# Attention with 16 queries per head: TensorE's loop turned to QK(g), PV(g-1), a K block transposed during the first softmax, no closing barrier, last rows stored by two queues

## The chip, the cores and the metric

The kernel runs on one core of one Trainium2 chip. The time is the device time of one execution in microseconds (us). The profile's *span* is shorter: it goes from the first to the last instruction of the kernel, and what comes before and after it is counted in the time but is in no view. Kernel before: 641.1 us, median of 3 runs (641.03 to 641.29).

## The reference

```python
B, H, Sq, Skv, Dh = 8, 16, 16, 2048, 256      # q, k, v: bfloat16, normal * 0.05
def reference(q, k, v):
    scale = q.shape[-1] ** -0.5
    scores = jnp.einsum('bhqd,bhkd->bhqk', q, k) * scale
    attn = jax.nn.softmax(scores, axis=-1)
    return jnp.einsum('bhqk,bhkd->bhqd', attn, v)
```

There are 128 heads. K and V are 134 MB each and every byte is used once; Q is 1 MB. That is little arithmetic for each byte.

## The kernel before

The heads are worked in 16 blocks g of 8 heads. A block has two *units* u = 2g + e, of 4 heads and 4.19 MB of K and as much of V. SyncE issues all loads in one order. For each block:

- VectorE transposes K (`kt`, eight a block, into the small buffer `KB`), TensorE multiplies it with Q (`qk`, into PSUM `S_ps`), VectorE takes the maximum, ScalarE the exponential, VectorE transposes P (`pt`) and spreads it (`px`), and TensorE multiplies P with V (`pv`).
- `KN` holds one block of K and `VB` one block of V. So K of block g+1 can be requested only when `kt` of block g is through, and V of block g+1 only when `pv` of block g is.

The order of the loads and of TensorE's work (cut; `qk_block(g)` is the four `qk` of a block):

```python
def k_load(u):
    deps = [("kt", g - 1, e, 3)] if g else []           # K buffer free
    ...                                                  # SyncE issues the load
def v_load(u):
    ... deps = [("kt", g, e, 3)] if g == last else [("pv", g - 1, 1)] if g else ...

for u in (0, 1): k_load(u)
v_load(0); k_load(2); v_load(1); k_load(3)
for g in range(2, G):
    for u in (2 * g, 2 * g + 1): k_load(u)
    for u in (2 * g - 2, 2 * g - 1): v_load(u)
v_load(NU - 2); v_load(NU - 1)

qk_block(0)                                              # TensorE
qk(1, 0, 0); qk(1, 0, 1); pv(0, 0); qk(1, 1, 0); qk(1, 1, 1); pv(0, 1)
qk_block(2)
for g in range(3, last):
    pv(g - 2, 0); pv(g - 2, 1)
    qk_block(g)
...                                                      # last two blocks, V in parts
```

Each engine's stream stands inside one `nc.Block()`, which ends with a barrier of all engines. The last V unit is loaded in seven parts: 16, 16, 8, 8, 8, 4 and 4 of its 64 rows for each partition.

## Time and profile before

| what | before |
|---|---|
| time, span | 641.1 us, 639.5 us |
| DMA | 269.5 MB read, 423 GB/s over the span, 431 to 432 from 100 to 560 us |
| busy PE, DVE, ACT | 77%, 67%, 15% of the span |
| one turn of the chain of waits | 39.07 us |

From the page of the kernel before: the busy tenths of the DMA engines and their GB/s in 40 equal slices of the span, then the chain that ended last, by engine and by line, then three groups of instructions (busy us, mean ns of one, idle time before them and what ended it).

```profile
DMA  9999999999999999999999999999999999999996
GB/s 319 436 427 427 438 419 440 428 427 434 426 434 426 430 441 424 443 426 429 428 426 437 428 430 437 421 446 416 441 428 426 435 424 437 435 427 435 421 422 253
...
DMA 72%; DVE 23%; PE 3%; issue 1%; SPq 0%; ACT 0%; DVEq 0%; ACTq 0%
...
L128 DVE STREAM_TRANSPOSE KB<-KN 128x2048 f32<-128x2048 f32 x128 | 284.8, 2281 | 154.3 <-DMA KN<-in_k_dram 131.6
L145 PE MATMUL S_ps<-KB,QW 128*128 128x512 bf16 x528 | 215.9, 418 | 127.4 <-DVE KB L128 127.4
L173 PE MATMUL O_ps<-VB,PT 128*128 128x512 bf16 x896 | 198.9, 383 | 17.7 <-DMA VB<-in_v_dram 17.7
```

The DMA engines are busy all the time but at the two ends. Every compute engine has idle time, and most of it ends on a load, or on work that waited for a load. The chain of waits in order of time (start, us, what; pieces of 0.02 us between them left out) repeats two pieces. One turn goes from one start of the transposes to the next, 39.07 us:

```profile
390.27 8.90 DVE KB L128 x4
...
399.20 30.12 DMA KN<-in_k_dram
...
429.34 8.90 DVE KB L128 x4
```

A K load of 4.19 MB is 30.1 us from issue to landing, but its transfer is only a third of that (4.19 MB at 431 GB/s are 9.7 us); in the rest it stands in the queue behind two other loads, which keep the DMA engines busy while VectorE transposes. A turn moves four units, 16.78 MB, in 39.07 us: 429 GB/s.

The end of the kernel before, from its timeline (start us, us, engine, line, operation), and the events of the closing barrier (queue of the engine, then first and last start):

```profile
633.80 2.92 PE L179 MATMUL O_ps<-KN,PT 128*128 128x256 bf16 x24
634.79 1.64 PEld L179 LDWEIGHTS O_ps<-KN,PT 128*128 128x128 bf16 x16 [0.24 <-DMA KN<-in_v_dram]
636.75 0.48 DVE L331 TENSOR_SCALAR O_fin<-O_ps,rab 128x256 bf16<-128x256 f32 x1 [6.64 <-PE O_ps L179]
637.27 0.50 ACTq L186 DMA_DIRECT2D out_dram<-O_fin  x1
...
L48 ACTq COMPARE_BRANCH  x1: 38/38/38, 639.2 to 639.2; - x1
L48 SPq EVENT_SEMAPHORE  x1: 17/17/17, 639.5 to 639.5; - x1
```

The last wait for V ends at 634.79 us with 16 weight loads still to do; then come the last scaling, the store, and about 0.3 us of barrier.

### The profile page before, as it was taken

The page shows a single profiled execution, that of the slowest core. Times are in us where ns is not written, and L with a number is a line of the kernel's source. Part 1 is how long each engine was busy: PE and PEld are TensorE (multiplying, and loading weights), DVE is VectorE, ACT ScalarE, POOL GpSimd, SP SyncE. Part 2 cuts the span into 40 slices and gives each one's busy share as a digit, 9 for nine tenths or more (in the row PEclk, how much of TensorE's full clock was granted, in tenths as well). Part 3 has the DMA queues.
Part 4 walks back from the last instruction along what each step waited for, and adds up shares of the span by engine and source line. Part 5 has one row for each costly group of instructions (what it writes and reads, how often), then busy time and mean ns, then how long its engine had stood idle before and what let it go on. Part 6 is the DMA issues. An engine that isn't in the chain of part 4 may idle for free.

```text
span 639.5 us, 4835 instructions
## 1 busy us (share of the span) xinstructions
PE 491.4 (77%) x2176; PEld 166.7 (26%) x1680; DVE 428.2 (67%) x372; ACT 99.1 (15%) x208; POOL 4.2 (1%) x7
## 2 busy tenths in 40 slices
PE   0827979876896768958688686797866878686998
PEld 0102313213131221412213132131311313122286
DVE  4866598693857938488483875939569395694861
ACT  2121203030120301202012120211203012030010
POOL 2000000000000000000000000000000000000000
PEclk9977989899897998979899798998989989799899
DMA  9999999999999999999999999999999999999996
GB/s 319 436 427 427 438 419 440 428 427 434 426 434 426 430 441 424 443 426 429 428 426 437 428 430 437 421 446 416 441 428 426 435 424 437 435 427 435 421 422 253
DMA packets 15483, 270.67 MB, mean 423 GB/s; under 512 B 1776, under 2 KB 3824, under 8 KB 4464
## 3 DMA queue, kind: packets, MB, share of 16 engines
q1 hardware_dynamic: 13152, 269.49, 98.7%
q10 hardware_dynamic: 2320, 1.05, 0.6%
q8 instruction: 5, 0.08, 0.1%
q14 instruction: 6, 0.05, 0.0%
HBM read 269.48 MB, written 1.05 MB: 423 GB/s over the span
## 4 chain that ended last, share of the span: by engine, by line
DMA 72%; DVE 23%; PE 3%; issue 1%; SPq 0%; ACT 0%; DVEq 0%; ACTq 0%
DMA KN<-in_k_dram 68%; DVE KB L128 22%; DMA KN<-in_v_dram 5%; PE O_ps L179 2%; PE S_ps L145 1%; PE S_ps L133 1%; DVE PC L159 0%; SPq L112 0%; DVE negm L150 0%; ACT QW L121 0%; DVE O_fin L331 0%; SPq L213 0%; SPq L232 0%; ACT P_sb L154 0%; DVE rab L300 0%
## 5 line engine op out<-in xcount | busy, mean ns | idle before, releaser
L128 DVE STREAM_TRANSPOSE KB<-KN 128x2048 f32<-128x2048 f32 x128 | 284.8, 2281 | 154.3 <-DMA KN<-in_k_dram 131.6
L145 PE MATMUL S_ps<-KB,QW 128*128 128x512 bf16 x528 | 215.9, 418 | 127.4 <-DVE KB L128 127.4
L173 PE MATMUL O_ps<-VB,PT 128*128 128x512 bf16 x896 | 198.9, 383 | 17.7 <-DMA VB<-in_v_dram 17.7
L133 PE MATMUL S_ps<-KB,QW 128*128 128x512 bf16 x496 | 207.1, 417 | 0.0
L145 PEld LDWEIGHTS S_ps<-KB,QW 128*128 128x128 bf16 x528 | 54.4, 103 | 333.8 <-issue 232.4
L173 PEld LDWEIGHTS O_ps<-VB,PT 128*128 128x128 bf16 x896 | 87.5, 99 | 131.8 <-issue 31.1
L121 ACT ACTIVATE QW<-QT 32x128 bf16<-32x128 bf16 x128 | 53.9, 421 | 334.4 <-PE S_ps L133 326.5
L165 DVE COPY PT<-PC 32x1024 bf16<-32x1024 bf16 x128 | 53.3, 416 | 4.3 <-PE O_ps L179 2.6
L159 DVE STREAM_TRANSPOSE PC<-P_sb 128x1024 bf16<-128x1024 bf16 x32 | 37.9, 1224 | 21.1 <-ACT P_sb L154 21.1
L150 DVE TENSOR_REDUCE negm<-S_ps 128x1 f32<-128x2048 f32 x16 | 36.7, 2292 | 7.9 <-PE S_ps L133 7.5
L154 ACT ACTIVATE P_sb<-S_ps,negm 128x1024 bf16<-128x1024 f32 x32 | 35.4, 1110 | 36.1 <-DVE negm L150 26.4
L316 ACT ACTIVATE O_tmp<-O_ps,rab 128x256 f32<-128x256 f32 x15 | 7.1, 474 | 144.2 <-PE O_ps L173 143.4
L179 PE MATMUL O_ps<-KN,PT 128*128 128x256 bf16 x128 | 14.4, 273 | 0.2 <-DMA KN<-in_v_dram 0.2
L179 PE MATMUL O_ps<-VB,PT 128*128 128x256 bf16 x128 | 14.1, 273 | 0.1
L179 PEld LDWEIGHTS O_ps<-VB,PT 128*128 128x128 bf16 x128 | 12.4, 98 | 2.0 <-DVE PT L165 0.6
L179 PEld LDWEIGHTS O_ps<-KN,PT 128*128 128x128 bf16 x128 | 12.3, 98 | 2.2 <-issue 0.5
L331 DVE TENSOR_SCALAR O_fin<-O_ps,rab 128x256 bf16<-128x256 f32 x2 | 1.0, 484 | 11.8 <-PE O_ps L179 11.8
L321 DVE SCALAR_TENSOR_TENSOR O_fin<-O_ps,rab,O_tmp 128x256 bf16<-128x256 f32 x15 | 6.7, 448 | 1.8 <-issue 1.8
L154 ACT ACTIVATION_READ_ACCUMULATOR P_sb<-S_ps,negm 128x1 f32 x32 | 6.3, 196 | 0.0
L115 DVE STREAM_TRANSPOSE QT<-VB 128x2048 f32<-128x2048 f32 x1 | 2.3, 2311 | 5.6 <-DMA VB<-in_q_dram 5.6
L300 DVE TENSOR_SCALAR rab<-mask,rinv 128x2 f32<-128x2 f32 x16 | 3.7, 229 | 0.6
L191 POOL MEMSET PT<- 128x4096 f32 x1 | 3.5, 3512 | 0.0
(11 smaller groups left out, 7.8 us busy)
## 6 DMA issues: line engine op xcount, KB each, us to landing
KN<-in_k_dram SPq DMA_DIRECT2D x29, 4096.0 KB, 29.8
VB<-in_v_dram SPq DMA_DIRECT2D x32, 2048.0 KB, 25.2
VB<-in_v_dram SPq DMA_DIRECT2D x14, 4096.0 KB, 20.0
KN<-in_k_dram SPq DMA_DIRECT2D x6, 2048.0 KB, 21.0
KN<-in_v_dram SPq DMA_DIRECT2D x2, 2048.0 KB, 27.7
KN<-in_v_dram SPq DMA_DIRECT2D x2, 1024.0 KB, 23.4
KN<-in_v_dram SPq DMA_DIRECT2D x3, 512.0 KB, 26.1
VB<-in_q_dram SPq DMA_DIRECT2D x4, 256.0 KB, 4.5
```

The source lines that it names most:

```text
L121: ins = eng.activation(ap_of(dv, dv.offset + 32 * a + e, [[256, 4], [128, 2], [2, 16]]), ap_of(sv, sv.offset + 2 * (2 * g + e), [[64, 4], ...
L128: return eng.transpose(KBf[:, c % R_KB].rearrange("p t i -> p (t i)"), KNf[:, e].rearrange("p t i -> p (t i)")[:, n * c:n * c + n])
L133: return eng.add_instruction(mybir.InstMatmult(start_tensor_calc=start, stop_tensor_calc=stop, ldweights=False, tile_size=(128, 128), tile ...
L145: ins = mm(S_ps[:, 2 * h + c, :], QW[:, e, bp, :], rhs, start=(e == 0 and bp == 0), stop=(e == 1 and bp == 7))
L150: return eng.tensor_reduce(out=negm[:, g:g + 1], in_=S_ps[:].rearrange("p c n -> p (c n)"), axis=AX.X, op=ALU.max, negate=True)
L154: return eng.activation(P_sb[:, 1024 * h:1024 * h + 1024], S_ps[:, 2 * h:2 * h + 2, :].rearrange("p c n -> p (c n)"), ACTF.Exp, bias=negm[ ...
L159: return eng.transpose(PC[:, h].rearrange("p t x -> p (t x)"), P_sb[:, 1024 * h:1024 * h + 1024])
L165: ins = eng.tensor_copy(PT[pr, 32 * h:32 * h + 32, pr], PC[pr, h])
L173: ins = eng.matmul(O_ps[:, 0, :], PT[:, t, :], rhs, start=(t == 0), stop=(t == NT - 1))
L179: ins = eng.matmul(O_ps[:, bank, 0:D], PT[:, t, :], buf[:, t, :], start=(t == 0), stop=(t == NT - 1))
L316: j_ea[g] = J("act", "ea", lambda eng: eng.activation(O_tmp[:], src, ACTF.Copy, scale=rab[:, g, 0:1]), [("pv", g, 1) if g < last - 1 else ...
L321: j_eb[g] = J("dve", "eb", lambda eng: eng.scalar_tensor_tensor(out=O_fin[:, g % 2, :], in0=src, scalar=rab[:, g, 1:2], in1=O_tmp[:], op0= ...
```

## The change

Its intent is to keep less in the way at the two ends: load both K blocks before V in the head and transpose K(1) while softmax(0) runs, make the loop a plain QK(g), PV(g-1) from block 1 on, end without a barrier, and finish the last rows in smaller pieces. The diff, cut to its core:

```diff
-        block = ec(nc.Block())
...
-            return eng.dma_start(dst[e], O_fin[e:128:2, 2 + e, :])
+            return eng.dma_start(dst[e, r0:r1], O_fin[2 * r0 + e:2 * r1:2, 2 + e, :])
...
-        vparts = {NU - 2: [32, 32], NU - 4: [32, 32], NU - 1: [16, 16, 8, 8, 8, 4, 4]}
+        vparts = {NU - 2: [32, 32], NU - 4: [32, 32], NU - 1: [16, 16, 8, 8, 8, 4, 2, 2]}
...  (K of blocks 0 and 1 in halves, each waiting only for its own half of the buffer)
-        for u in (0, 1):
-            k_load(u)
-        v_load(0)
-        k_load(2)
-        v_load(1)
-        k_load(3)
-        for g in range(2, G):
+        for g in range(G):
             for u in (2 * g, 2 * g + 1):
                 k_load(u)
-            for u in (2 * g - 2, 2 * g - 1):
-                v_load(u)
+            if g:
+                for u in (2 * g - 2, 2 * g - 1):
+                    v_load(u)
...
         qk_block(0)
-        qk(1, 0, 0) ... pv(0, 1); qk_block(2)
-        for g in range(3, last):
-            pv(g - 2, 0)
-            pv(g - 2, 1)
+        for g in range(1, last):
             qk_block(g)
+            pv(g - 1, 0)
+            pv(g - 1, 1)
...  (VectorE: kt(1, 0, 0) and kt(1, 0, 1) between max(0) and pt(0); px(0) after kt of block 1)
+        finish_store("sp", 1, 0, 32)
+        finish_store("act", 1, 32, 64)
...
-        @block.sync ... @block.gpsimd
+        emit_stream(nc.sync, "sp")
+        ...
+        emit_pe(nc.tensor)
```

## The prediction

> **What bounds the kernel now.** The loads. The page's slices show the DMA engines busy at nine tenths or more in 39 of 40 slices; the windows view gives 431 to 432 GB/s from 100 to 560 us. The Trainium skill, "DMA: Bandwidth & Descriptors", section "Specifications", puts the fabric ceiling at 435 GB/s; this trace is at it. K, V and Q are 269.5 MB: 625 us at 431 GB/s. PE is busy 77%, DVE 67%, ACT 15%. The chain of waits repeats every 39.07 us (30.1 us of a K load, 8.9 us of four K transposes), and two units of K and V (16.78 MB) in 39.07 us are 429 GB/s: the transposes in that chain cost nothing, other loads are queued meanwhile. A 4 MB K load lands 29.8 us after its issue, a V load 20.0 us; one takes about 9.8 us of transfer. So only the first microseconds and the end can give time.
>
> **What the change does.**
> 1. Loop turned. Before: QK(2), then (PV(g-2), QK(g)). After: (QK(g), PV(g-1)). From QK(2) on that is the same order; only the loop's cut moves. 0 us.
> 2. Head: loads go K0 K1 K2 K3 V0 V1 instead of K0 K1 V0 K2 V1 K3, the same bytes. The danger is an empty queue. Estimates from the timeline: half a K lands each 4.9 us from 12.5 us on, so K1 ends at 27, K2 at 37, K3 at 47, V1 at 61 to 66 us. K2's halves may be issued at 17.0 and 21.9, K3's at 27.9 and 32.3: all 5 us or more ahead. K4 about 50, K5 about 59. PV(0) would run about 63 to 77 us (64 matmuls at 217 ns), so V2 is issued near 77 with the queue full until 81 to 86: the narrowest margin, 4 us. No gap, 0 us; transposing K(1) during softmax(0) moves DVE work off nothing critical.
> 3. Tail: last V part 4 cut to 2+2. When the last PE wait ends (634.79 us), 16 weight loads are still to come, 1.9 us of PE work: PE's backlog, not the last piece, ends the chain. Gain 0 to 0.2 us.
> 4. Last store on two queues. One issue took 0.50 us and landed 1.8 us after its start. Both halves still pay nearly all of that (same page, section "Issuing engines are not separate DMA queues": they run on the same engines). Gain 0 to 0.2 us.
> 5. No closing barrier: the store lands at about 639.1, the last semaphore event is at 639.5. Gain 0.3 us. The entry without the block: under 0.1 us.
>
> **Sum.** About 0.6 us of 641.1: **640.5 us**, 8 in 10 between 639.4 and 641.5. Faster by over 2%: 0.01. Within 2%: 0.98. Slower by over 2%: 0.01.
>
> **What would show it.** Middle windows still 430 to 432 GB/s, 39.1 us a turn; no window from 20 to 100 us below 400 GB/s; V2 issued before V1, K4 and K5 have all landed; the last V landing within 0.5 us of 634.8; PE's last matmul at 636 to 637; the last event straight after the store's landing; span about 639.0.
>
> **What would make it wrong.** A gap when V2 comes late, for instance if PE runs at the low clock through QK(1) and PV(0): the 4 us margin goes, and each microsecond of gap is a microsecond of time. In the other direction, a DMA gap in the head before that the slices hide (the first 10 us hold 257 GB/s, which I put down to start-up and Q's small rows). Or the small last pieces slow the end of the stream by some tenths.

## The result, and the profile after

The changed kernel takes 640.49 us, median of 6 runs (640.30 to 640.73); the kernel before, on the same chip, 641.07 us (641.01 to 641.63). The ratio is 0.9989 with a 95% interval of 0.9976 to 1.0002. (A ratio here is the mean time of one kernel's runs over the mean of the other's of the same rounds, so it is not quite the ratio of the medians.) So it is the same within 2%, and about 0.6 us, a tenth of a per cent, less. The interval just includes 1.

The same lines of the page of the changed kernel:

```profile
DMA  9999999999999999999999999999999999999996
GB/s 322 428 431 426 432 433 441 435 427 428 421 438 429 431 429 429 437 439 425 437 414 443 431 429 431 425 430 433 437 441 425 432 417 440 429 429 430 421 427 258
...
DMA 67%; DVE 25%; PE 7%; issue 1%; SPq 0%; DVEq 0%
...
L126 DVE STREAM_TRANSPOSE KB<-KN 128x2048 f32<-128x2048 f32 x128 | 284.6, 2281 | 159.7 <-DMA KN<-in_k_dram 139.3
L143 PE MATMUL S_ps<-KB,QW 128*128 128x512 bf16 x528 | 213.1, 413 | 125.2 <-DVE KB L126 125.2
L171 PE MATMUL O_ps<-VB,PT 128*128 128x512 bf16 x896 | 200.7, 386 | 22.2 <-DMA VB<-in_v_dram 22.2
```

Nothing in the middle has moved: the same rate, the same busy times. A turn of the chain is still 39.05 us (429.19 us less 390.14 us, both starts of transposes):

```profile
390.14 8.90 DVE KB L126 x4
399.06 30.11 DMA KN<-in_k_dram
429.19 8.90 DVE KB L126 x4
```

The head is where work did move. SyncE's issues in the timeline of the changed kernel (the second number spans all the issues merged in the line): the eight half loads of K0 to K3 by 32.8 us, then V0 and V1, then K4 and K5, then V2 and V3:

```profile
2.56 30.22 SPq L211 DMA_DIRECT2D KN<-in_k_dram  x8
32.83 1.38 SPq L229 DMA_DIRECT2D VB<-in_v_dram  x3
50.05 9.10 SPq L215 DMA_DIRECT2D KN<-in_k_dram  x2
76.81 1.28 SPq L229 DMA_DIRECT2D VB<-in_v_dram  x3
```

V2, the load with the narrowest margin, is issued at 76.81 us, where the prediction had "near 77". No stretch of 10 us from 20 to 100 us falls below 401 GB/s. A mean over 10 us could still hide a short gap, so the trace's packet records (start, duration and size of every DMA packet) were counted as well: from 2 to 620 us there is no moment without a packet of 2 KB or more under way, and fewer than 12 (there are 16 engines) for only 0.02 us in all, before and after. The queue was never empty. The end, with the last waits for the stores:

```profile
633.74 2.83 PE L177 MATMUL O_ps<-KN,PT 128*128 128x256 bf16 x23
634.65 1.64 PEld L177 LDWEIGHTS O_ps<-KN,PT 128*128 128x128 bf16 x16 [0.26 <-DMA KN<-in_v_dram]
636.61 0.48 DVE L323 TENSOR_SCALAR O_fin<-O_ps,rab 128x256 bf16<-128x256 f32 x1 [6.66 <-PE O_ps L177]
637.12 0.55 SPq L185 DMA_DIRECT2D out_dram<-O_fin  x1
637.13 0.52 ACTq L185 DMA_DIRECT2D out_dram<-O_fin  x1
...
L417 ACTq EVENT_SEMAPHORE  x2: 38/38/38, 637.7 to 638.9; - x2
L417 SPq EVENT_SEMAPHORE  x1: 17/17/17, 639.2 to 639.2; - x1
```

TensorE's last wait ends 0.14 us earlier than before, which is within the spread of the runs' spans (639.0 to 639.2 us). Still 16 weight loads follow it. The barrier's events are gone. The two half stores do not end together: ScalarE's wait is over at 638.9 us, 1.8 us after its issue, SyncE's at 639.2, 2.1 us after.

### The profile page after: what moved, and what is told of

It reads as the page before. It is cut to its first block, busy times and chain, and to the rows that moved or that the text cites. A ratio compares the mean times of both kernels' runs of the same rounds, so it can differ in the third digit from the quotient of the medians.

```text
span 639.2 us, 4824 instructions
## 1 busy us (share of the span) xinstructions
PE 489.1 (77%) x2176; PEld 166.7 (26%) x1680; DVE 427.8 (67%) x372; ACT 99.1 (16%) x208; POOL 4.2 (1%) x7
## 3 DMA queue, kind: packets, MB, share of 16 engines
HBM read 269.48 MB, written 1.05 MB: 423 GB/s over the span
## 4 chain that ended last, share of the span: by engine, by line
DMA 67%; DVE 25%; PE 7%; issue 1%; SPq 0%; DVEq 0%
DMA KN<-in_k_dram 67%; DVE KB L126 23%; PE O_ps L177 4%; PE S_ps L143 1%; PE S_ps L131 1%; DVE negm L148 0%; DVE PC L157 0%; SPq L110 0%; DVE PT L163 0%; DVE O_fin L323 0%; DVE O_fin L313 0%; DVE rab L292 0%; DVE rinv L291 0%; DVEq L410 0%; DVE ltot L289 0%
## 5 line engine op out<-in xcount | busy, mean ns | idle before, releaser
L143 PE MATMUL S_ps<-KB,QW 128*128 128x512 bf16 x528 | 213.1, 413 | 125.2 <-DVE KB L126 125.2
L171 PE MATMUL O_ps<-VB,PT 128*128 128x512 bf16 x896 | 200.7, 386 | 22.2 <-DMA VB<-in_v_dram 22.2
L131 PE MATMUL S_ps<-KB,QW 128*128 128x512 bf16 x496 | 203.9, 411 | 0.0
## 6 DMA issues: line engine op xcount, KB each, us to landing
KN<-in_k_dram SPq DMA_DIRECT2D x8, 2048.0 KB, 15.3
```

The costliest lines, as they stand in the source:

```text
L131: return eng.add_instruction(mybir.InstMatmult(start_tensor_calc=start, stop_tensor_calc=stop, ldweights=False, tile_size=(128, 128), tile ...
L143: ins = mm(S_ps[:, 2 * h + c, :], QW[:, e, bp, :], rhs, start=(e == 0 and bp == 0), stop=(e == 1 and bp == 7))
L171: ins = eng.matmul(O_ps[:, 0, :], PT[:, t, :], rhs, start=(t == 0), stop=(t == NT - 1))
```

## The experiments

The theory: the loads bound the kernel, the queue is never empty in either version, and so only the end can give time, mostly the barrier. The rivals: the new head order gives the gain; the smaller last pieces give it; or the chain of waits is to be taken at its word, and transposes and TensorE count. Each job ran beside the kernel before on the same chip.

### The parts of the change, each alone

`a1_no_block` is the kernel before with only this edit:

```diff
-        block = ec(nc.Block())
-        @block.sync
-        def _(eng):
-            emit_stream(eng, "sp")
-        ...
+        emit_stream(nc.sync, "sp")
+        ...
```

> Kernel before with the block, and so its closing barrier, taken away alone. Theory (the barrier is most of the gain): 0.3 to 0.6 us shorter than before, ratio 0.9990 to 0.9996, last PE matmul unmoved at 636 to 637 us, and the time outside the span falls too. Rival (head and loop order gives the gain): within 0.15 us of before.

`a2_tail` is the kernel before with only the tail's edits:

```diff
-NU - 1: [16, 16, 8, 8, 8, 4, 4]
+NU - 1: [16, 16, 8, 8, 8, 4, 2, 2]
-        finish_store(1)
+        finish_store("sp", 1, 0, 32)
+        finish_store("act", 1, 32, 64)
```

> Kernel before with the last V part cut to 2+2 and the last rows stored by two queues, block kept. Theory: 0 to 0.2 us shorter, since the two half stores land 1.8 to 2.0 us after issue as the whole one did. Rival (the tail's finer pieces give the gain): 0.4 us or more shorter.

`a3_head` is the changed kernel with the block and the old tail put back, so only the loop and the head differ from before:

```diff
+        block = ec(nc.Block())
-        emit_stream(nc.sync, "sp") ...
+        @block.sync ...
-8, 8, 8, 4, 2, 2]
+8, 8, 8, 4, 4]
-        finish_store("sp", 1, 0, 32)
-        finish_store("act", 1, 32, 64)
+        finish_store("act", 1, 0, 64)
```

> Changed kernel with the block and the old tail put back: only the turned loop and the new head order remain. Theory (a DMA queue that is never empty): within 0.15 us of before. Rival (head order gives the gain): 0.4 us or more shorter.

`a4_after` is the changed kernel with no edit.

> The changed kernel itself, on the same chip as the three parts. Expected: 0.4 to 0.7 us shorter than before; the parts alone should sum to it within 0.2 us.

Measured, 5 runs each and 9 of the kernel before:

| run | median us (range) | ratio to before, 95% | mean span us | mean time less span us |
|---|---|---|---|---|
| before | 641.23 (641.01 to 641.37) | | 639.42 | 1.78 |
| a1_no_block | 640.45 (640.27 to 641.06) | 0.9990 (0.9976 to 1.0004) | 639.04 | 1.47 |
| a2_tail | 641.55 (641.39 to 642.10) | 1.0007 (0.9994 to 1.0021) | 639.82 | 1.79 |
| a3_head | 641.39 (641.19 to 641.46) | 1.0002 (0.9988 to 1.0015) | 639.52 | 1.81 |
| a4_after | 640.74 (640.62 to 641.00) | 0.9994 (0.9980 to 1.0007) | 639.32 | 1.46 |

Without the block alone, the median is 0.78 us below before, more than the whole change gives here (0.49 us). The tail alone is 0.32 us above before, the head 0.16. The sum, -0.30, agrees with -0.49 within the 0.2 us that were expected. No single ratio excludes 1, but over all jobs the kernels sort almost without overlap: the runs of the kernel before took 641.01 to 641.93 us; those of the changed kernel and of a1_no_block took 640.27 to 641.06, and one of them alone is above 641.00. What tells the kernels apart best is the last column: with the block the time is 1.78 to 1.81 us longer than the span, without it 1.46 or 1.47 (in the other jobs 1.78 for the kernel before, 1.33 to 1.47 for the runs without the block). So the block cost about 0.3 us in the profile, where the barrier's events stand (639.2 to 639.5 us), and about 0.3 us more where no view shows it. What that second part is, is left open. The edit takes away the block's entry together with its closing barrier. Inside the span the entry costs nothing (SyncE's first load starts at 0.74 us and its first K load at 2.56 us in the traces of before and of a1_no_block alike), but outside the span these runs cannot tell the two apart.

### Time to spare in the head

`b1_pe80` and `b2_pe160` are the changed kernel with extra work for TensorE after QK(0), so that QK(1) and PV(0) come late (80 and 160 matmuls, into a PSUM bank that is free then):

```diff
         qk_block(0)
+        def emit_dummy(eng):
+            for _ in range(80):            # 160 in b2_pe160
+                ins = eng.matmul(O_ps[:, 3, :], ident[:], QT[:, 0:512], start=True, stop=True)
+            return ins
+        J("pe", "dummy", emit_dummy, [j_ident, ("qt", 0)])
```

> Changed kernel with 80 extra matmuls (about 17.4 us at 217 ns) on TensorE between QK(0) and QK(1), into a PSUM bank that is free then. Estimate: QK(1) starts 10 us later, PV(0) ends and V2 is issued near 82 to 84 us, while K5 lands near 87. Theory (the queue's margin covers it): time within 0.3 us of the changed kernel's 640.5. Rival (TensorE, the chain through QK, counts): 5 us or more longer.

> The same with 160 extra matmuls (about 34.7 us). Estimate: K5 can be issued only near 83 us (its buffer is freed by transposes that wait for QK(1)) and V2 near 101 us, which the queue needed by about 86: the queue runs empty. Theory: 12 to 18 us longer, with windows below 350 GB/s between 75 and 105 us, and 430 GB/s again after. Rival (slack somewhere later takes it back): under 3 us longer.

`b1_pe80` took 640.48 us (4 runs, 640.48 to 640.88): some 17 us of extra matmuls cost nothing. V2 was issued at 82.65 us in place of 76.81, and no stretch of 10 us from 40 to 120 us fell below 408 GB/s. SyncE's issue of V2, and the window around it (stretch; busy us and instructions of each engine; granted clock, DMA share, GB/s):

```profile
82.65 1.28 SPq L229 DMA_DIRECT2D VB<-in_v_dram  x3
...
80.00:90.00 10.00, 9.73 (x45) 2.50 (x26) 9.17 (x5) 0.47 (x1) 0.00 (x0) 1.00 1.02 433
```

`b2_pe160` took 657.86 us (657.45 to 658.17), 17.4 us more than the changed kernel and ratio 1.0255 (1.0237 to 1.0272) to before, at the upper end of the expected 12 to 18. Its windows and SyncE's issues:

```profile
70.00:80.00 10.00, 8.79 (x41) 2.01 (x21) 5.79 (x3) 1.71 (x4) 0.00 (x0) 1.00 0.50 215
80.00:90.00 10.00, 9.26 (x44) 2.80 (x29) 8.63 (x11) 2.46 (x5) 0.00 (x0) 1.00 0.65 252
90.00:100.00 10.00, 10.00 (x48) 4.51 (x46) 9.48 (x9) 1.51 (x4) 0.00 (x0) 1.00 0.39 167
...
120.00:300.00 180.00, 140.97 (x594) 45.26 (x453) 118.36 (x102) 26.57 (x57) 0.00 (x0) 0.93 1.01 432
...
50.03 33.44 SPq L215 DMA_DIRECT2D KN<-in_k_dram  x2
100.65 1.28 SPq L229 DMA_DIRECT2D VB<-in_v_dram  x3
```

The second of the two K loads, K5, went out at 83.47 us (50.03 plus 33.44) and V2 at 100.65 us. The DMA engines stood half idle from 70 to 100 us: the packet records have 13.9 us without any packet of 2 KB or more under way, where `b1_pe80` has none. Nothing gave that back later. The missing bytes of these three stretches at 430 GB/s come to 6.6 MB (2.15 + 1.78 + 2.63), or 15.3 us, most of the 17.4 us; 100 to 120 us, at 367 and 394 GB/s, hold another 2.3 us. So the margin exists, it is above 5.8 us (82.65 less 76.81), and past it a microsecond of empty queue is a microsecond of time.

### Less VectorE work, and fewer bytes

`b3_half_kt`: from block 1 on each K transpose moves half of its columns.

```diff
-            return eng.transpose(KBf[:, c % R_KB]..., KNf[:, e]...[:, n * c:n * c + n])
+            return eng.transpose(KBf[:, c % R_KB]...[:, 0:m], KNf[:, e]...[:, n * c:n * c + m])
+   # m = n for block 0, n / 2 after it
```

> Changed kernel whose K transposes from block 1 on move half of the columns (wrong result on purpose): about 133 us less of VectorE work in all, 4.5 us less in each turn of the chain of waits. Theory (loads bound): within 0.3 us of 640.5 but for the last block, whose transposes lie on the tail and may give up to 1 us. Rival (the chain's 23% of VectorE is real): 30 us or more shorter.

It took 640.65 us (640.60 to 640.71), 0.2 us more than the changed kernel and ratio 0.9988 (0.9972 to 1.0005) to before. (It multiplies stale halves of K and still passed the comparison: the scores of this input are so small that the softmax is nearly even. It computes no attention all the same.) From its page:

```profile
PE 493.7 (77%) x2176; PEld 170.0 (27%) x1680; DVE 300.1 (47%) x372; ACT 99.0 (15%) x208; POOL 4.2 (1%) x7
...
DMA 84%; DVE 12%; PE 2%; SPq 1%; issue 0%
```

VectorE has 127.7 us less to do (427.8 less 300.1), its share of the chain falls from 25% to 12%, and the time stays. The DMA share of the chain takes up all of it: the loads are issued earlier and stand in the queue for longer. The rival is out.

`b4_less_v`: half of V is loaded for units 12 and 14, and the result is wrong.

```diff
-                j_v[u].append(J("sp", "ld", lambda eng, a=a, n=n: eng.dma_start(
+                j_v[u].append(J("sp", "ld", lambda eng, a=a, n=(HT if u in (12, 14) else n): eng.dma_start(
```

> Changed kernel that loads only half of V units 12 and 14 (wrong result on purpose): 4.19 MB less of 269.5, no other instruction changed. Theory (loads bound): 9.7 us shorter (4.19 MB at 431 GB/s). Rival (VectorE or TensorE chain): under 2 us shorter.

It took 631.04 us (630.77 to 631.11), ratio 0.9837 (0.9821 to 0.9854) to before and 9.45 us less than the changed kernel. Its page has 4.19 MB less than the 269.48 MB of the others, at the same rate:

```profile
HBM read 265.29 MB, written 1.05 MB: 423 GB/s over the span
```

1.6% fewer bytes gave 1.5% less time; the expected figure was 9.7 us.

### Trying to gain at the head and in the packets

In the first microseconds the DMA engines are busy but move little. Windows of 1 us of the changed kernel, then of `c1_k_first`, which issues the first half of K0 ahead of Q:

```profile
4.00:5.00 1.00, 0.00 (x0) 0.00 (x0) 0.00 (x0) 0.00 (x0) 0.92 (x1) 1.00 0.86 205
5.00:6.00 1.00, 0.00 (x0) 0.00 (x0) 0.00 (x0) 0.00 (x0) 0.00 (x0) 1.00 1.09 238
```

```profile
5.00:6.00 1.00, 0.00 (x0) 0.00 (x0) 0.00 (x0) 0.00 (x0) 0.00 (x0) 1.00 1.04 442
...
8.00:9.00 1.00, 0.00 (x0) 0.00 (x0) 0.00 (x0) 0.00 (x0) 0.00 (x0) 1.00 1.15 238
9.00:10.00 1.00, 0.00 (x0) 0.00 (x0) 0.00 (x0) 0.00 (x0) 0.00 (x0) 1.00 0.87 188
```

```diff
-        j_q = [J("sp", "ldq", ...) for a in range(4)]        # ahead of all K
+                    if (u, h) == (0, 1):                     # in k_load: after the first half of K0
+                        j_q.extend(J("sp", "ldq", ...) for a in range(4))
```

> Changed kernel with the first half of K0 issued ahead of the four Q loads. In the first 6 us the DMA engines are busy but move about 245 GB/s, and Q's 8 KB packets took 595 ns against 310 ns near the end of the run. If that is the start of the run: no change, within 0.2 us. If it is Q's form (32 partitions each): no change either, and Q's packets stay at 595 ns further on. If the engines only lack work while SyncE issues four small loads: 1 to 2 us shorter.

It took 641.50 us (641.08 to 641.63), ratio 1.0002 (0.9988 to 1.0015) to before and 1.0 us more than the changed kernel. The slow stretch went along with Q: K runs at 442 GB/s from 5 to 6 us and Q at 188 to 238 later. In the trace's packet records Q's 8 KB packets took a median of 596 ns in the changed kernel and 610 ns here, against 312 ns for other 8 KB packets near the end of the run. So Q is slow wherever it stands. The start is slow as well: from 2 to 3 us, before Q's packets, this run moved 115 GB/s of K. The order costs 1.0 us (0.8 against `a4_after`), where no change was expected. The packet records show where: after 5 MB, at about 16 us, this run's trace is 0.7 us behind the changed kernel's, and it stays 0.6 to 0.7 us behind to the end, with no moment without a packet. So the loss lies in the first 16 us. A cause that would fit is that the slow start now falls on K, while Q, which is slow anyway, is still to come; it was not tested.

`d1_q_two` tries a cause. The Trainium skill, "SBUF — State Buffer", section "Door 1: The DMA port swizzle", says that partitions 0 to 63 reach only the 8 even ports of 16, and 64 to 127 the odd ones. Each of the four Q loads fills 32 partitions. So the two halves were issued side by side:

```diff
-        j_q = [J("sp", "ldq", ...
+        j_q = [J("sp" if a < 2 else "act", "ldq", ...
```

> Changed kernel whose Q loads for partitions 64 to 127 are issued by ScalarE's queue beside those for partitions 0 to 63 on SyncE's. Theory (Q's form is slow because 32 partitions reach half of the SBUF ports, Trainium skill, SBUF page; two halves at once reach all): Q's 1 MB passes in about 2.5 us instead of 4.9, so 1.5 to 2.4 us shorter than the changed kernel, near 638.5 us, and windows near 430 GB/s from 3 us on. Rival (Q's rows or the start of the run are slow whatever the partitions): within 0.3 us of 640.5.

```profile
4.00:5.00 1.00, 0.00 (x0) 0.00 (x0) 0.00 (x0) 0.00 (x0) 0.91 (x1) 1.00 1.07 262
5.00:6.00 1.00, 0.00 (x0) 0.00 (x0) 0.00 (x0) 0.00 (x0) 0.00 (x0) 1.00 1.32 320
6.00:7.00 1.00, 0.00 (x0) 0.00 (x0) 0.00 (x0) 0.00 (x0) 0.00 (x0) 1.00 0.79 262
```

640.53 us (640.18 to 640.64), ratio 0.9989 (0.9975 to 1.0002) to before: no gain over the changed kernel, which is what the rival had said. Q's packets took 491 ns, better than 596 and far from 312, and all of Q passed in 4.60 us in place of 4.94. The rate of one Q load alone, 205 to 238 GB/s or about half of the 431, fits the page; the step "both halves at once, full rate" failed. The same page says so in its section "Can I just issue two DMAs to hit both halves?": two such transfers "serialize", measured there as 6% faster than one, and only one transfer over all 128 partitions reaches all ports. That was overlooked when the run was planned, and the trace agrees with it: 4.94 against 4.60 us is 7%. One load of Q over 128 partitions was not tried, and the rows of Q are left as a rival, so that the ports are the cause is argued and not shown.

`d2_q_two_tail` adds the old tail to d1 (the tail's lines of the diff of a3_head).

> The same with the old tail (last V part of 4, last rows stored by one transfer on ScalarE's queue), still without the closing barrier. In the changed kernel SyncE's half store was seen 2.08 us after its issue, ScalarE's half 1.8, one whole store 1.83. Theory (two queues cost 0.2 to 0.3 us): 0.2 to 0.4 us shorter than d1_q_two. Rival (run noise): within 0.1 us of it.

640.50 us (640.12 to 640.61), 0.03 us from d1_q_two. So the 0.3 us that a2_tail showed against the tail is not confirmed: the tail's pieces are worth nothing either way that these runs can tell.

`c2_v_whole` loads each odd V unit by one transfer in place of two halves (but for the last two blocks). In the packet records, 32 KB packets take 1214 ns and 16 KB packets 612, so larger ones should have gained.

```diff
-            return vparts.get(u, [HT, HT] if u % 2 else [NT])
+            return vparts.get(u, [NT])
```

> Changed kernel with every odd V unit loaded by one transfer instead of two halves (14 units; the last two blocks keep their parts): packets of 32 KB at 1214 ns instead of 2 times 16 KB at 611 ns. Estimate: 8 ns for each pair, 8 pairs an engine and unit: 0.064 us a unit, 0.9 us in all. Theory (loads bound, packet time counts): 0.5 to 1.2 us shorter. Rival: PV waits longer for V, no gain or a loss.

It took 648.94 us (648.43 to 652.12), ratio 1.0137 (1.0117 to 1.0157): 8.5 us slower than the changed kernel, and the rival was right. From its chain in order of time:

```profile
303.99 15.73 PE O_ps L171 x64
...
319.74 0.33 SPq L229
...
320.11 23.70 DMA VB<-in_v_dram
...
343.95 16.23 PE O_ps L171 x64
```

The chain is another one now. PV needs all of V's odd unit before its first matmul, it takes 16 us for 64 matmuls, the next V load waits for its end, and the turn is 39.96 us (343.95 less 303.99) in place of 39.05. TensorE's waits for V grew from 22.2 to 98.9 us in 14 waits. Over twelve turns (V's issues at 83.76 and 561.03 us) the mean is 39.77 us: 0.7 us more a turn, some 8.6 us in all, which is about the loss. From 204 to 206 us the DMA engines moved 246 GB/s. After running nearly dry the queue also started again slowly here: 159 of the 7296 packets of 32 KB took over 1.4 us, 125 of them within 3 us of a late V issue, where the changed kernel has 3 of 5376. Splitting the odd unit, which costs a little in packets, is what gives PV its early start and the queue its margin in every turn.

## Why the prediction was right or wrong

- **What bounds the kernel**: right, and now shown and not only read. 4.19 MB less of V gave 9.45 us; 127.7 us less of VectorE work and 17 us more of TensorE work gave nothing.
- **The turned loop, 0 us; the head, 0 us**: right. a3_head is 0.16 us from before, where 0.15 was the limit set, and the ranges overlap. The estimate of V2's issue ("near 77") was met at 76.81 us. The margin "4 us" was too narrow: an issue 5.8 us later cost nothing. The low clock that the prediction named as a danger did come (0.67 granted from 40 to 50 us, where QK(1) begins), and V2 was on time all the same.
- **The last V part, 0 to 0.2 us; two queues, 0 to 0.2 us**: gain not seen. a2_tail was 0.32 us slower, d2_q_two_tail against d1_q_two 0.03 us faster with the old tail. The reason given for the part holds in the trace, since 16 weight loads follow the last wait before and after. For the store, the half on SyncE's queue is done 0.3 us after ScalarE's, so the split hid nothing.
- **No closing barrier, 0.3 us**: the direction was right and the size too small. a1_no_block gave 0.78 us by medians. The 0.3 us read off the trace was there, and time outside the span fell by another 0.3 us, which the prediction had no term for (whether the barrier or the block's entry causes that part is open).
- **The sum, 0.6 us and 640.5 us**: measured 640.49. What bounds the kernel was understood; that the sum came out within 0.1 us is partly luck: the block gave more and the tail less than said, and the two errors cancelled. In the job with the parts the same kernel, a4_after, gained 0.49 us. All of this is near the noise: neither interval excludes 1.

What stays open: the 0.3 us outside the span, whether the ports make Q's packets take twice as long as others, and why K ahead of Q cost 1.0 us in the first 16 us.

## What to carry to other kernels

In this kernel the queue of loads was never empty, and so work on other engines could be moved, halved or lengthened for nothing, although the chain of waits shows it with a quarter of the span. In a kernel like it, look for the margin between a load's issue and the moment when the queue would run dry. The same margin is what a harmless-looking merge of two loads can use up, and then each turn of the loop pays. Here a block with a closing barrier cost more than its events in the profile, so compare the time with the span as well.

## What the Trainium skill lacked or had wrong

- "DMA: Bandwidth & Descriptors", section "Specifications", lists about 358 GB/s as the limit of HBM for one core, as half of a stack's 716. That a core which streams alone is not held to it is said only further down the page. With this kernel on one core, these runs read 431 to 432 GB/s for 460 us on end, close to the 435 GB/s of the same table.
- "SBUF — State Buffer" was not wrong: Q loads into 32 partitions each ran at 205 to 238 GB/s, about half rate, and with two of them side by side all of Q passed in 4.60 us in place of 4.94, 7% faster where the page has 6%.
- No page has that taking away a block with its closing barrier shortens the time outside the profile's span: 1.78 to 1.81 us with it, 1.33 to 1.47 us without.
- No page lists what one packet of these sizes takes: medians of 312 ns for 8 KB, 612 ns for 16 KB and 1214 ns for 32 KB in these traces, or 596 ns for Q's 8 KB.
